# Attention and two MoE layers in one program: head pairs interleaved over partitions, filler products at the start, one half-block slice

## The chip, the core and the metric

The program runs on one core of a Trainium2 chip. Its engines work side by side, each through its own instructions in order: TensorE (PE; PEld is its weight load), VectorE (DVE), ScalarE (ACT), GpSimd (POOL) and SyncE (SP, which here only issues DMAs). They wait for each other by semaphores. The metric is the device time of one execution in microseconds.

## The reference

Four batches of eight heads attend in chunks of 32 queries: each chunk sees 8 memory slots, 16 keys to its left, its own 32 and 8 to its right. Two expert layers without routing follow.

```python
for c in range(nc):                                   # attention, chunk by chunk
    k_full = np.concatenate([mem_k, k_ctx], axis=2)   # 8 + up to 56 keys
    scores = scale * np.matmul(q_c, k_full.transpose(0, 1, 3, 2))
    a = np.exp(scores - scores.max(-1)); a = a / (a.sum(-1) + 1e-9)
    out[:, :, chunk] = np.matmul(a, v_full)
x = out as (3072 tokens, 512)
h = np.maximum(x @ w_in, 0);  x = (s * h * h + b) @ w_out        # d_ff 2048
h = x @ w_in2;  out = (h * sigmoid(1.702 * h)) @ w_out2
```

## The kernel before

**Attention.** The 3072 tokens are 24 tiles of 128. `attend(t)` (line 368) builds one tile's steps. It loads `q` (line 380) and, with two DMAs each, `kbd` and `vbd` (line 384): these hold the keys and values of two heads block by block, head 0 of a pair on partitions 0 to 63 in half 0 of the tile, head 1 on 64 to 127 in half 1, and the other two quarters are zeros, filled once at the start (line 248). So one product with 128 rows gives the scores of both heads: 16 small products (line 392). VectorE takes the maximum (`top`, line 405) and subtracts it (`less`, line 409), ScalarE exponentiates (line 414), TensorE transposes (`pp`, line 419), the result is copied to `pt` (line 211), 16 products give the values (`o`, line 436), VectorE sums and inverts (`total`, lines 427 to 429) and scales to `xn` (line 442), TensorE transposes back (`xx`, line 448), and the block's input is split in a high and a low part, `xh` (line 211) and `xl` (line 460). Four tiles make a block of 512 tokens, six blocks in all.

**The two layers.** Weights come as 64-bit words in 32 column blocks per layer (16 `w_in`, 16 `w_out`); `prep` (line 295) loads one into `st` (line 304) and takes it apart into a high part (`wih`, `woh`) and a low part (`wil`, `wol`) on ScalarE and VectorE (lines 311 to 342). `step` (line 521) takes one column block j for one block of tokens: 12 hidden products into `ph` (lines 537 to 539), the gate on ScalarE and VectorE (lines 545 to 569), 12 output products into `acc` (line 584). The first `LEAD` = 2 column blocks of block 0 are done in halves of 256 tokens: first half (tiles 0 and 1) of j=0 and j=1, then second half (tiles 2 and 3) of both. `VISITS` then sets which blocks pass which j; block 1 follows block 0's first five.

**Order.** `Plan` (line 46) holds every step with its engines, durations and dependences, and lays them out in time on a model of the engines; the order in which it picks them is the order in which the instructions are written. Buffers with tags delay a step until an earlier holder's users are done. `plan.op` makes each step that takes a tagged buffer wait for the step that took it last. In line 271 ten products of a zero tile with itself (`warm`) are put first on TensorE.

Of the kernel before, what the change touches and what calls it, by code (L numbers as in the profile page):

```python
# [32 lines left out]
WARM = 10  # L33
LEAD = 2
NLATE = 4
# [10 lines left out]
class Plan:  # L46


    DMA_START, DMA_END = 1.1, 1.0

    def __init__(self):
        self.ops, self.users, self.tags, self.last, self.soon = [], {}, {}, {}, set()

# [3 lines left out]
    def op(self, need, engines, fn, after=(), alloc=(), uses=()):  # L57
        n = len(self.ops)
        after = list(after)
        for tag, _ in alloc:  # L60
            if tag not in ("a0", "u"):
                if tag in self.last:
                    after.append(self.last[tag])
                self.last[tag] = n
        self.ops.append((need, engines, fn, after, list(alloc), list(uses)))
        for h in uses:
            self.users.setdefault(h, []).append(n)
        return n

    def order(self):  # L70
# [8 lines left out]
        dma_free = 0.0  # L79
        waits = [len(o[3]) for o in ops]  # L80
        outs = [[] for _ in ops]
        for i, o in enumerate(ops):
            for d in o[3]:
                outs[d].append(i)
# [6 lines left out]
        for i in range(len(ops) - 1, -1, -1):  # L91
            need, engines = ops[i][:2]
            due = [late[o] - min(engines.values()) - WAKE for o in outs[i]]
            if "pe" in engines or not due:
                due = [marks[min(bisect.bisect_left(marks, (need, -1.0)), len(marks) - 1)][1]] if "pe" in engines else [
                    marks[min(bisect.bisect_left(marks, (need, -1.0)), len(marks) - 1)][1] - min(engines.values())]
            if i in self.soon:
                due.append(marks[min(bisect.bisect_left(marks, (need, -1.0)), len(marks) - 1)][1])
            late[i] = min(due)

# [9 lines left out]
        def ready(i, e):  # L110
            t = max(free[e], free["act"]) if e == "aq" else free[e]
            for d in ops[i][3]:
                gap = 0.0 if (ran[d] == e and e in ("pe", "sp")) else WAKE
                t = max(t, ends[d] + (gap if e != "none" else 0.0))
            for tag, _ in ops[i][4]:
                bufs, given = self.tags[tag]
                if len(given) >= bufs:
                    h = given[-bufs]
                    for u in self.users.get(h, ()):
                        if ends[u] is None:  # L120
                            return None
                        t = max(t, ends[u] + WAKE)
            return t
# [49 lines left out]
        self.span = max(ends)  # L173
        return chosen


@with_exitstack
def attention_moe_moe(ctx: ExitStack, tc: tile.TileContext, q_t, k_w, v_w, w_in1, w_out1, s_b, w_in2, w_out2, out):
# [26 lines left out]

    plan = Plan()
    op = plan.op
    T = {}
# [46 lines left out]
    o_cold = op(-999, {"dve": 0.2}, chill, alloc=[("r", "cold")])  # L255
    o_ident = op(-200, {"pool": 0.5}, lambda e: make_identity(nc, ident))
    o_zero = {}
    for i in range(2):
        for n in range(2):
            o_zero[i, n] = [  # L260
                op(-150 + 10 * i + n, {"dve": 1.1}, lambda e, x=kvs[i][n][0:64, 1]: fill(e, x, 0.0)),
                op(-150 + 10 * i + n, {"pool": 0.9}, lambda e, x=kvs[i][n][64:128, 0]: fill(e, x, 0.0)),
            ]
# [28 lines left out]
    o_open = {}  # L292
    last = {}

    def prep(i):
# [44 lines left out]
        def rest(e):  # L340
# [3 lines left out]
        st, u = ("st", i), ("u", i)  # L344
        a = op(need, {"sp": 1.9}, load, after=[last[x] for x in ("load",) if x in last], alloc=[("st", st)])
        c = op(need, {"act": 0.67}, low, after=[a], uses=[st])
        b = op(need, {"act": 0.67} if m == 0 else {"act": 0.67, "dve": 0.36}, absolute, after=[a] + [last[x] for x in ("abs",) if x in last] + o_open.get(pool, []),
               alloc=[("u", u), (pool + tag, w)], uses=[st])
# [5 lines left out]
        f = op(need, {"dve": 0.62}, rest, after=[d], uses=[u])  # L354
        last["load"], last["abs"] = a, b
        o_w[w] = (d, f)
# [11 lines left out]
    def attend(t):  # L368
# [13 lines left out]
        def load(x, src, j):  # L382
            h = slice(64 * j, 64 * j + 64)
            return lambda e: (nc.sync if e == "sp" else nc.scalar).dma_start(
                out=x[h, j].rearrange("p a c s -> p (a c s)"), in_=src[t, h])

# [20 lines left out]
        def less(e):  # L407
            T["e", t] = pool.tile([P, H, SLOTS], F32, tag="e", name="e")
            nc.vector.tensor_tensor(  # L409
                out=T["e", t], in0=T["sc", t], in1=T["top", t].to_broadcast([P, H, SLOTS]), op=ALU.subtract  # L410
            )
# [4 lines left out]
        def turn(e):  # L416
            pp = T["pp", t] = ps_a.tile([P, HP, P], F32, tag="a", name="pp")
            for a in range(HP):
                nc.tensor.transpose(pp[:, a, :], T["e", t][:, 2 * a:2 * a + 2, :].rearrange("p h s -> p (h s)"), ident)  # L419

# [4 lines left out]
        def total(e):  # L425
            den = T["den", t] = pool.tile([P, H, 1], F32, tag="den", name="den", bufs=2)
            nc.vector.tensor_reduce(out=den, in_=T["e", t], op=ALU.add, axis=AX.X)
            nc.vector.tensor_scalar_add(out=den, in0=den, scalar1=1e-9)
# [33 lines left out]
        ps, pt, pv, px = [at_a[f, t] for f in "STVX"]  # L462
        lq = op(ps, {"sp": 0.95}, load_q, alloc=[("q" + g, ("q", t))])
        war = [o_s[prior]] if prior is not None else []
        near = [] if t < 2 else [t - 2] if t <= max(EARLY) else [t - 2, t - 1] if t == max(EARLY) + 1 else [t - 1]
        turns, vals, backs = [[o[x] for x in near] for o in (o_t, o_v, o_b)]
        lk = [op(ps, {"aq" if j and t < 8 else "sp": 0.9 if t < 8 else 1.2}, load(kb, k_w, j), after=war) for j in range(2)]
        s = o_s[t] = op(ps, {"pe": 1.05}, scores, after=[lq] + lk + zk + turns, alloc=[("a0", ("sc", t))], uses=[("q", t)])
# [8 lines left out]
        war = [o_v[prior]] if prior is not None else []  # L477
        lv = [op(pv, {"aq" if j and t < 8 else "sp": 0.9 if t < 8 else 1.2}, load(vb, v_w, j), after=war) for j in range(2)]
        o = o_v[t] = op(pv, {"pe": 0.97}, values, after=[d] + lv + zv + backs, alloc=[("a0", ("o", t))], uses=[("pt", t)])
# [41 lines left out]
    def step(i):  # L521
# [72 lines left out]
        for k in range(KT):  # L594
            after = ready + (list(o_split[b, k]) if m else [])
            if d is not None:
                after.append(d)
            d = op(at_h[i], {"pe": dur}, hid(k), after=after, alloc=[("h", ("h", i))] if k == 0 else [],
                   uses=[("x", m, b), win])
# [92 lines left out]

    with tc.manual_schedule():
        for i, e in plan.order():
            plan.ops[i][2](e)
        for x in list(managers)[::-1]:
# [6 lines left out]
def _layouts(q, k, v, mem_k, mem_v, moe_w_in, moe_w_out, moe_s, moe_b, moe2_w_in, moe2_w_out):  # L703
# [17 lines left out]

    q_t = q.reshape(B, HP, 2, TPB, P, D).transpose(0, 3, 2, 5, 1, 4)
    k_w = windows(k, mem_k).transpose(0, 3, 2, 6, 1, 4, 5)
# [30 lines left out]
```

## Time and profile before

| | us |
|---|---|
| median of 3 runs (1158.6 to 1161.57) | 1158.94 |
| profiled execution | 1155.9 |
| its span, first to last instruction | 1154.1 |
| TensorE busy in the span | 1135.5 |
| VectorE busy | 554.4 |
| ScalarE busy | 449.5 |
| mean granted clock of TensorE | 0.989 |

Busy is the time in which an engine had an instruction under way; a product's record covers its pipeline, so neighbours overlap, and the pace is read from start to start. The granted clock is in shares of 2.4 GHz. A mean over the whole span hides its stages: attention of the first eight tiles and the first weights fill the first 80 us.

### The profile page before, as it was taken

What the parts mean: (1) busy time and instruction counts of PE and PEld (TensorE: products, weight loads), DVE (VectorE), ACT (ScalarE), POOL (GpSimd) and SP (SyncE); (2) the same over time, 40 slices, a digit from 0 to 9 for tenths busy, and PEclk for the clock granted to TensorE, in tenths of its full rate; (3) what the DMA queues carried; (4) which work ended last, traced back from release to release, by engine and by line L of the source; (5) the groups of instructions that cost most, each with busy time, mean ns of one, the idle gap of its engine ahead of it and who ended that gap; (6) DMA issues with size and microseconds to landing.
All of it is one profiled execution on the core that took longest, in us unless ns stands there. A gap on an engine that the chain in (4) does not pass through costs nothing.

```text
span 1154.1 us, 15714 instructions
## 1 busy us (share of the span) xinstructions
PE 1135.5 (98%) x6404; PEld 936.5 (81%) x6404; DVE 554.4 (48%) x991; ACT 449.5 (39%) x758; POOL 4.4 (0%) x10
## 2 busy tenths in 40 slices
PE   6899999999999999999999999999999999999998
PEld 5778888888888888888888888888888888888887
DVE  6799983444333434449999822324323223222221
ACT  3679764333334334345555332232222222222222
POOL 1000000000000000000000000000000000000000
PEclk6999999999999999999999999999999999999999
DMA  9974452323113214213444200111001000000000
GB/s 227 246 205 145 129 153 78 89 64 92 47 34 96 69 42 110 65 56 124 132 148 162 93 1 1 37 37 43 31 1 39 35 1 1 37 1 1 36 1 37
DMA packets 30647, 84.89 MB, mean 74 GB/s; under 512 B 3952, under 2 KB 3952, under 8 KB 30576
## 3 DMA queue, kind: packets, MB, share of 16 engines
q1 hardware_dynamic: 29296, 79.71, 23.9%
q10 hardware_dynamic: 1280, 4.20, 1.6%
q8 instruction: 50, 0.82, 0.3%
q14 instruction: 21, 0.17, 0.0%
HBM read 71.30 MB, written 12.58 MB: 73 GB/s over the span
## 4 chain that ended last, share of the span: by engine, by line
PE 94%; DMA 3%; DVE 1%; ACT 1%; issue 0%; SPq 0%; DVEq 0%; ACTq 0%
PE acc L584 44%; PE ph L537 15%; PE ph L538 15%; PE ph L539 15%; PE o L436 2%; PE sc L392 2%; DMA st<-w_in 1%; PE pp L419 1%; DMA st<-w_out 1%; PE xx L448 1%; DMA kbd<-k_w 1%; DMA q<-q_t 1%; DVE e L409 0%; DVE top L405 0%; ACT u L311 0%
## 5 line engine op out<-in xcount | busy, mean ns | idle before, releaser
L537 PE MATMUL ph<-xh,wih 128*128 128x512 f32 (+1 forms) x776 | 305.7, 394 | 0.0
L538 PE MATMUL ph<-xl,wih 128*128 128x512 f32 (+1 forms) x776 | 301.0, 388 | 0.0
L539 PE MATMUL ph<-xh,wil 128*128 128x512 f32 (+1 forms) x776 | 300.9, 388 | 0.0
L569 DVE TENSOR_TENSOR gl<-r,gh 128x512 fp32r<-128x512 f32 (+1 forms) x194 | 132.8, 684 | 213.8 <-ACT gh L565 213.6
L565 ACT CAST gh<-r 128x512 fp32r<-128x512 f32 (+1 forms) x194 | 119.9, 618 | 261.9 <-PE acc L584 250.8
L537 PEld LDWEIGHTS ph<-xh,wih 128*128 128x128 f32 x776 | 146.5, 189 | 33.1 <-issue 4.7
L539 PEld LDWEIGHTS ph<-xh,wil 128*128 128x128 f32 x776 | 146.2, 188 | 30.3 <-DVE wil L342 0.3
L538 PEld LDWEIGHTS ph<-xl,wih 128*128 128x128 f32 x776 | 146.5, 189 | 28.1
L561 DVE TENSOR_TENSOR r<-ph,r 128x512 f32<-128x512 f32 x96 | 66.3, 691 | 180.8 <-ACT r L547 180.5
L584 PE MATMUL acc<-gh,woh 128*128 128x512 f32 (+1 forms) x392 | 151.5, 386 | 0.0
L584 PE MATMUL acc<-gl,woh 128*128 128x512 f32 (+1 forms) x392 | 150.9, 385 | 0.2 <-DVE gl L569 0.2
L584 PE MATMUL acc<-gh,wol 128*128 128x512 f32 (+1 forms) x392 | 151.0, 385 | 0.0
L584 PE MATMUL acc<-woh,gh 128*128 128x512 f32 x384 | 149.4, 389 | 0.0
L584 PE MATMUL acc<-wol,gh 128*128 128x512 f32 x384 | 149.4, 389 | 0.0
L584 PE MATMUL acc<-woh,gl 128*128 128x512 f32 x384 | 149.4, 389 | 0.0
L547 ACT ACTIVATE r<-ph 128x512 f32<-128x512 f32 x96 | 57.4, 598 | 209.4 <-PE ph L539 208.6
L545 ACT ACTIVATE r<-ph 128x512 f32<-128x512 f32 (+1 forms) x98 | 57.8, 590 | 143.0 <-PE ph L539 136.6
L559 DVE TENSOR_SCALAR r<-r,sb 128x512 f32<-128x512 f32 x86 | 46.8, 545 | 118.0 <-ACT r L554 117.3
L584 PEld LDWEIGHTS acc<-gh,woh 128*128 128x128 f32 x392 | 73.6, 188 | 15.3 <-issue 0.8
L584 PEld LDWEIGHTS acc<-gl,woh 128*128 128x128 f32 x392 | 73.7, 188 | 14.9 <-DVE gl L569 0.4
L584 PEld LDWEIGHTS acc<-gh,wol 128*128 128x128 f32 x392 | 73.7, 188 | 14.6
L584 PEld LDWEIGHTS acc<-woh,gl 128*128 128x128 f32 x384 | 72.1, 188 | 15.0
(62 smaller groups left out, 891.5 us busy)
## 6 DMA issues: line engine op xcount, KB each, us to landing
st<-w_in SPq DMA_DIRECT2D x32, 512.0 KB, 3.5
st<-w_out SPq DMA_DIRECT2D x32, 512.0 KB, 3.9
kbd<-k_w SPq DMA_DIRECT2D x40, 256.0 KB, 4.9
vbd<-v_w SPq DMA_DIRECT2D x40, 256.0 KB, 4.2
q<-q_t SPq DMA_DIRECT2D x24, 256.0 KB, 5.2
xf<-y SPq DMA_DIRECT2D x6, 1024.0 KB, 5.2
out<-y SPq DMA_DIRECT2D x20, 256.0 KB, 2.2
y<-y SPq DMA_DIRECT2D x16, 256.0 KB, 2.1
```

What stands on the lines that cost most here:

```text
L392: nc.tensor.matmul(sc[r, 2 * a:2 * a + 2, :], T["q", t][:, a, r], kb[:, :, a, c, :], start=True, stop=True)
L436: nc.tensor.matmul(o[r, 2 * a:2 * a + 2, :], T["pt", t][:, a, r], vb[:, :, a, c, :], start=True, stop=True)
L537: nc.tensor.matmul(ph, wh, xh, start=(k == 0), stop=False)
L538: nc.tensor.matmul(ph, wh, xl, start=False, stop=False)
L539: nc.tensor.matmul(ph, wl, xh, start=False, stop=(k == KT - 1))
L545: nc.scalar.activation(out=a, in_=T["ph", i], func=AF.Relu)
L547: nc.scalar.activation(out=a, in_=T["ph", i], func=AF.Sigmoid, scale=GATE)
L559: nc.vector.tensor_scalar(out=a, in0=a, scalar1=sb[:, 0:1], scalar2=sb[:, 1:2], op0=ALU.mult, op1=ALU.add)
L561: nc.vector.tensor_tensor(out=a, in0=T["ph", i], in1=a, op=ALU.mult)
L565: nc.scalar.copy(out=T["g", i][0], in_=T["r", i])
L569: nc.vector.tensor_tensor(out=gl, in0=T["r", i], in1=gh.bitcast(F32), op=ALU.subtract)
L584: nc.tensor.matmul(o, lt, rh, start=fresh and x == 0, stop=(done and x == 2))
```

## The change

1. **Interleaving.** Head 0 of a pair now lies on the even partitions and head 1 on the odd ones, in `q`, `kbd`, `vbd` and the transposed exponents. The loads write every second partition (`x[j::2, j]`), the zero fill covers all 128 partitions of both halves, and the loads of tiles 0 and 1 wait for it. To have the transposes come out interleaved, the tile `e` is stored with the two heads alternating word by word: `less` writes it in steps of two words, `total` reads it so.
2. **Fillers.** Where the plan leaves TensorE idle before the first hidden product, products of the zero tile with itself are written, one per 0.24 us of the planned gap.
3. **LEAD = 1.** Only j=0 of block 0 is done in two halves.
4. **The plan.** A step with a tagged buffer no longer waits for the end of the step that took it last, only for its start; loads and first steps of different weights are no longer chained; planned durations of loads change, the zero fills and the identity get other due times, and the `vbd` loads of tiles 0 and 1 are all issued by SyncE.

```diff
-LEAD = 2
+LEAD = 1
...
+    BEAT = 0.24
...
-        after = list(after)
+        behind = []
         for tag, _ in alloc:
             if tag not in ("a0", "u"):
                 if tag in self.last:
-                    after.append(self.last[tag])
+                    behind.append(self.last[tag])
                 self.last[tag] = n
...
                 t = max(t, ends[d] + (gap if e != "none" else 0.0))
+            for d in ops[i][6]:
+                t = max(t, starts[d])
...
-        return chosen
+        full, clock = [], 0.0
+        for i, e in chosen:
+            if e == "pe":
+                idle = min(starts[i], starts[self.first]) - clock
+                if idle > 0.3:
+                    full.append((None, int(idle / self.BEAT)))
+                clock = ends[i]
+            full.append((i, e))
+        return full
...
-                op(-150 + 10 * i + n, {"dve": 1.1}, lambda e, x=kvs[i][n][0:64, 1]: fill(e, x, 0.0)),
-                op(-150 + 10 * i + n, {"pool": 0.9}, lambda e, x=kvs[i][n][64:128, 0]: fill(e, x, 0.0)),
+                op(-150 + 10 * i + n, {"dve": 1.1}, lambda e, x=kvs[i][n][:, 1]: fill(e, x, 0.0)),
+                op(-150 + 10 * i + n, {"pool": 0.9}, lambda e, x=kvs[i][n][:, 0]: fill(e, x, 0.0)),
...
-        a = op(need, {"sp": 1.9}, load, after=[last[x] for x in ("load",) if x in last], alloc=[("st", st)])
+        a = op(need, {"sp": 1.55}, load, alloc=[("st", st)])
...
-                out=x[h, j].rearrange("p a c s -> p (a c s)"), in_=src[t, h])
+                out=x[j::2, j].rearrange("p a c s -> p (a c s)"), in_=src[t, h])
...
-            T["e", t] = pool.tile([P, H, SLOTS], F32, tag="e", name="e")
+            T["e", t] = pool.tile([P, HP, SLOTS, 2], F32, tag="e", name="e")
             nc.vector.tensor_tensor(
-                out=T["e", t], in0=T["sc", t], in1=T["top", t].to_broadcast([P, H, SLOTS]), op=ALU.subtract
+                out=T["e", t].rearrange("p a s h -> p a h s"), in0=T["sc", t].rearrange("p (a h) s -> p a h s", h=2),
+                in1=T["top", t].rearrange("p (a h) o -> p a h o", h=2).to_broadcast([P, HP, 2, SLOTS]), op=ALU.subtract
...
-            nc.vector.tensor_reduce(out=den, in_=T["e", t], op=ALU.add, axis=AX.X)
+            nc.vector.tensor_reduce(
+                out=den.rearrange("p (a h) o -> p a (h o)", h=2), in_=T["e", t].rearrange("p a s h -> p a h s"), op=ALU.add, axis=AX.X)
...
-        lk = [op(ps, {"aq" if j and t < 8 else "sp": 0.9 if t < 8 else 1.2}, load(kb, k_w, j), after=war) for j in range(2)]
+        lk = [op(ps, {"aq" if j and t < 8 else "sp": 0.8}, load(kb, k_w, j), after=war + (zk if t < 2 else [])) for j in range(2)]
...
         for i, e in plan.order():
-            plan.ops[i][2](e)
+            if i is not None:
+                plan.ops[i][2](e)
+                continue
+            if idle is None:
+                idle = ps_acc.tile([P, 512], F32, tag="acc3", name="idle")
+            for _ in range(e):
+                nc.tensor.matmul(idle[:, :P], T["cold"], T["cold"], start=True, stop=True)
...
-    q_t = q.reshape(B, HP, 2, TPB, P, D).transpose(0, 3, 2, 5, 1, 4)
+    q_t = q.reshape(B, HP, 2, TPB, P, D).transpose(0, 3, 5, 2, 1, 4)
```

**The order that comes of it.** First place: TensorE from the program's start to the scores of tile 2. Before (`kbd_93` and `kbd_95` are the two key tiles, used by even and odd tiles; numbers tell buffers apart):

```order
L269 MATMUL warm_106<-cold_99 128x128 x10
L392 MATMUL sc_151<-kbd_93,q_117 32x128 x16
L392 MATMUL sc_179<-kbd_95,q_124 32x128 x16
L419 MATMUL pp_200<-ident_91,e_176 128x128 x4
L436 MATMUL o_215<-vbd_94,pt_210 32x128 x16
L419 MATMUL pp_239<-ident_91,e_213 128x128 x4
L436 MATMUL o_255<-vbd_96,pt_249 32x128 x16
L448 MATMUL xx_275<-ident_91,xn_251 128x128 x4
L448 MATMUL xx_288<-ident_91,xn_282 128x128 x4
L392 MATMUL sc_296<-kbd_93,q_170 32x128 x16
```

After, the same stretch to the second tile's values (the two transposes back and the scores of tile 2 follow, with three fillers between each):

```order
L717 MATMUL idle_105<-cold_99 128x128
L282 MATMUL warm_107<-cold_99 128x128 x10
L717 MATMUL idle_105<-cold_99 128x128 x9
L403 MATMUL sc_162<-kbd_93,q_102 32x128 x16
L717 MATMUL idle_105<-cold_99 128x128 x8
L403 MATMUL sc_206<-kbd_95,q_121 32x128 x16
L431 MATMUL pp_230<-ident_91,e_195 128x128 x4
L717 MATMUL idle_105<-cold_99 128x128 x10
L449 MATMUL o_262<-vbd_94,pt_238 32x128 x16
L431 MATMUL pp_285<-ident_91,e_249 128x128 x4
L717 MATMUL idle_105<-cold_99 128x128 x5
L449 MATMUL o_309<-vbd_96,pt_294 32x128 x16
```

The attention steps stand in the same order; 39 fillers stand among them, 10 before the first scores.

Second place: SyncE's first loads. Before:

```order
L304 DMA st_102<-w_in1 128x1024
L380 DMA q_117<-q_t 128x512
L384 DMA kbd_93<-k_w 64x1024
L380 DMA q_124<-q_t 128x512
L384 DMA kbd_95<-k_w 64x1024
L384 DMA vbd_94<-v_w 64x1024
L384 DMA vbd_96<-v_w 64x1024
```

After:

```order
L391 DMA q_102<-q_t 128x512
L316 DMA st_118<-w_in1 128x1024
L391 DMA q_121<-q_t 128x512
L395 DMA kbd_93<-k_w 64x1024
L316 DMA st_127<-w_out1 128x1024
L395 DMA kbd_95<-k_w 64x1024
L316 DMA st_136<-w_in1 128x1024
L395 DMA vbd_94<-v_w 64x1024 x2
```

The first key load moves from third to fourth, the second weight from ninth to fifth, and a third weight is put ahead of the first values. On ScalarE's queue stood two key and two value halves; there now stand the two key halves.

Third place: VectorE from the first `xl` of block 0 on. Before (`st_139` is the second weight, `st_237` the third):

```order
L460 TENSOR_TENSOR xl0_285<-xx_275,xh0_284 128x4x128
L460 TENSOR_TENSOR xl0_285<-xx_288,xh0_284 128x4x128
L342 TENSOR_TENSOR wol_245<-u_246,woh_244 128x512
L405 TENSOR_REDUCE top_322<-sc_296 128x8
L409 TENSOR_TENSOR e_331<-sc_296,top_322 128x512
L317 TENSOR_SCALAR u_340<-u_340 128x512
L405 TENSOR_REDUCE top_367<-sc_342 128x8
L325 TENSOR_SCALAR u_340<-u_340 128x512
L409 TENSOR_TENSOR e_374<-sc_342,top_367 128x512
L329 ISA u_340<-st_237,u_340 128x1024
```

After (`st_136` is the third weight, `st_181` the fourth):

```order
L345 SCALAR_TENSOR_TENSOR u_245<-st_136,u_245 128x512
L473 TENSOR_TENSOR xl0_339<-xx_329,xh0_338 128x4x128
L329 TENSOR_SCALAR u_302<-u_302 128x512
L473 TENSOR_TENSOR xl0_339<-xx_345,xh0_338 128x4x128
L354 TENSOR_TENSOR wil_244<-u_245,wih_243 128x512
L416 TENSOR_REDUCE top_388<-sc_359 128x8
L337 TENSOR_SCALAR u_302<-u_302 128x512
L420 TENSOR_TENSOR e_402<-sc_359,top_388 128x4x2x64
L341 ISA u_302<-st_181,u_302 128x1024
L416 TENSOR_REDUCE top_425<-sc_404 128x8
```

VectorE reaches the second `xl` with the third weight nearly done and the fourth begun; before, it finished the second there.

## Rows read from the trace of the kernel before

**Rows 1.** The page, part 1: busy us, share of the span, instructions.

```profile
PE 1135.5 (98%) x6404; PEld 936.5 (81%) x6404; DVE 554.4 (48%) x991; ACT 449.5 (39%) x758; POOL 4.4 (0%) x10
```

**Rows 2.** Windows: us, busy by engine (x instructions), granted clock, DMA share, GB/s.

```profile
10.00:20.00 10.00, 7.00 (x102) 5.43 (x98) 5.30 (x12) 2.31 (x4) 0.00 (x0) 0.50 1.06 233
...
50.00:60.00 10.00, 9.37 (x108) 7.40 (x109) 9.65 (x24) 7.24 (x15) 0.00 (x0) 1.00 0.97 265
...
60.00:80.00 20.00, 18.69 (x230) 14.80 (x229) 18.45 (x37) 15.16 (x27) 0.00 (x0) 1.00 0.84 222
...
300.00:600.00 300.00, 300.00 (x1864) 246.76 (x1857) 165.17 (x314) 126.56 (x212) 0.00 (x0) 1.00 0.30 85
```

**Rows 3.** Timeline of TensorE: start us, us, engine, line, operation, out<-in, idle before.

```profile
1.06 4.64 PE L269 MATMUL warm<-cold 128*128 128x128 f32 x20 [1.06 <-DVE cold L248]
...
9.85 1.93 PE L392 MATMUL sc<-kbd,q 128*32 128x128 f32 x32 [4.15 <-DMA kbd<-k_w]
...
27.70 0.58 PE L537 MATMUL ph<-xh,wih 128*128 128x256 f32 x1
...
30.31 1.08 PE L392 MATMUL sc<-kbd,q 128*32 128x128 f32 x32
...
43.25 0.28 PE L537 MATMUL ph<-xh,wih 128*128 128x256 f32 x1
...
44.69 0.28 PE L537 MATMUL ph<-xh,wih 128*128 128x256 f32 x1
...
47.23 0.39 PE L584 MATMUL acc<-gh,woh 128*128 128x256 f32 x1
...
81.73 0.48 PE L537 MATMUL ph<-xh,wih 128*128 128x512 f32 x1
...
90.01 0.39 PE L537 MATMUL ph<-xh,wih 128*128 128x512 f32 x1
...
95.45 0.39 PE L537 MATMUL ph<-xh,wih 128*128 128x512 f32 x1
```

**Rows 4.** Windows, the microsecond in which the clock comes back.

```profile
29.00:30.00 1.00, 1.00 (x7) 1.00 (x7) 0.59 (x2) 0.69 (x3) 0.00 (x0) 0.53 1.06 236
```

**Rows 5.** Timeline of VectorE.

```profile
11.89 0.17 DVE L399 MEMSET sc<- 32x128 f32 x1 [2.57 <-PE sc L392]
...
25.97 0.69 DVE L460 TENSOR_TENSOR xl<-xx,xh 128x512 fp32r<-128x512 f32 x1 [0.18 <-ACT xh L211]
...
41.55 1.28 DVE L460 TENSOR_TENSOR xl<-xx,xh 128x512 fp32r<-128x512 f32 x2
...
80.59 1.28 DVE L460 TENSOR_TENSOR xl<-xx,xh 128x512 fp32r<-128x512 f32 x2
```

**Rows 6.** Lines by form, VectorE, 0 to 84 us: busy, mean ns, idle before.

```profile
L333 DVE SCALAR_TENSOR_TENSOR u<-st,u 128x512 uint32<-128x512 uint32 x10 | 6.8, 676 | 0.1
...
L409 DVE TENSOR_TENSOR e<-sc,top 128x512 f32<-128x512 f32 x9 | 6.1, 683 | 0.1
...
L325 DVE TENSOR_SCALAR u<-u 128x512 uint32<-128x512 uint32 x11 | 4.6, 420 | 0.1
...
L248 DVE MEMSET kbd<- 64x1024 f32 x2 | 1.8, 912 | 0.3 <-issue 0.3
...
L399 DVE MEMSET sc<- 32x128 f32 x2 | 0.3, 165 | 2.7 <-PE sc L392 2.6
...
L248 DVE MEMSET cold<- 128x128 f32 x1 | 0.2, 165 | 0.8 <-PEq L743 0.8
```

**Rows 7.** Windows: attention loads alone, then weights alone.

```profile
300.00:310.00 10.00, 10.00 (x91) 8.38 (x84) 6.14 (x11) 3.13 (x6) 0.00 (x0) 1.00 0.56 131
...
600.00:610.00 10.00, 10.00 (x46) 8.27 (x45) 8.42 (x18) 6.17 (x12) 0.00 (x0) 1.00 0.62 212
```

**Rows 8.** Chain of waits: start us, us, what; tile 0's first key load.

```profile
1.66 8.05 DMA kbd<-k_w
```

**Rows 9.** Line 384, 0 to 45 us: landing of the key and value loads.

```profile
DMA to landing us min/median/max: 5.6/8.7/10.3
```

More of the change, by code (lines that the diff above doesn't have):

```diff
@@ L49 @@
     DMA_START, DMA_END = 1.1, 1.0
+    BEAT = 0.24
     def __init__(self):
-        self.ops, self.users, self.tags, self.last, self.soon = [], {}, {}, {}, set()
+        self.ops, self.users, self.tags, self.last, self.soon, self.due = [], {}, {}, {}, set(), {}
     def tag(self, name, bufs):
@@ L62, in op @@
                 if tag in self.last:
-                    after.append(self.last[tag])
+                    behind.append(self.last[tag])
                 self.last[tag] = n
-        self.ops.append((need, engines, fn, after, list(alloc), list(uses)))
+        self.ops.append((need, engines, fn, list(after), list(alloc), list(uses), behind))
         for h in uses:
@@ L79, in order @@
         dma_free = 0.0
-        waits = [len(o[3]) for o in ops]
+        waits = [len(o[3]) + len(o[6]) for o in ops]
         outs = [[] for _ in ops]
         for i, o in enumerate(ops):
-            for d in o[3]:
+            for d in o[3] + o[6]:
                 outs[d].append(i)
@@ L98, in order @@
                 due.append(marks[min(bisect.bisect_left(marks, (need, -1.0)), len(marks) - 1)][1])
-            late[i] = min(due)
+            late[i] = self.due.get(i, min(due))
         def push(i):
@@ L206, in attention_moe_moe @@
     plan = Plan()
+    plan.first = None
     op = plan.op
@@ L255, in attention_moe_moe @@
     o_cold = op(-999, {"dve": 0.2}, chill, alloc=[("r", "cold")])
-    o_ident = op(-200, {"pool": 0.5}, lambda e: make_identity(nc, ident))
+    plan.due[o_cold] = -1000.0
+    o_ident = op(-135, {"pool": 0.5}, lambda e: make_identity(nc, ident))
     o_zero = {}
@@ L292, in attention_moe_moe @@
     o_open = {}
-    last = {}
     def prep(i):
@@ L344, in prep @@
         st, u = ("st", i), ("u", i)
-        a = op(need, {"sp": 1.9}, load, after=[last[x] for x in ("load",) if x in last], alloc=[("st", st)])
+        a = op(need, {"sp": 1.55}, load, alloc=[("st", st)])
         c = op(need, {"act": 0.67}, low, after=[a], uses=[st])
-        b = op(need, {"act": 0.67} if m == 0 else {"act": 0.67, "dve": 0.36}, absolute, after=[a] + [last[x] for x in ("abs",) if x in last] + o_open.get(pool, []),
+        b = op(need, {"act": 0.67} if m == 0 else {"act": 0.67, "dve": 0.36}, absolute, after=[a] + o_open.get(pool, []),
                alloc=[("u", u), (pool + tag, w)], uses=[st])
@@ L354, in prep @@
         f = op(need, {"dve": 0.62}, rest, after=[d], uses=[u])
-        last["load"], last["abs"] = a, b
         o_w[w] = (d, f)
@@ L418, in turn @@
             for a in range(HP):
-                nc.tensor.transpose(pp[:, a, :], T["e", t][:, 2 * a:2 * a + 2, :].rearrange("p h s -> p (h s)"), ident)
+                nc.tensor.transpose(pp[:, a, :], T["e", t][:, a].rearrange("p s h -> p (s h)"), ident)
         def turned(e):
@@ L462, in attend @@
         ps, pt, pv, px = [at_a[f, t] for f in "STVX"]
-        lq = op(ps, {"sp": 0.95}, load_q, alloc=[("q" + g, ("q", t))])
+        lq = op(ps, {"sp": 0.8}, load_q, alloc=[("q" + g, ("q", t))])
         war = [o_s[prior]] if prior is not None else []
@@ L477, in attend @@
         war = [o_v[prior]] if prior is not None else []
-        lv = [op(pv, {"aq" if j and t < 8 else "sp": 0.9 if t < 8 else 1.2}, load(vb, v_w, j), after=war) for j in range(2)]
+        lv = [op(pv, {"aq" if j and 2 <= t < 8 else "sp": 0.8}, load(vb, v_w, j), after=war + (zv if t < 2 else [])) for j in range(2)]
         o = o_v[t] = op(pv, {"pe": 0.97}, values, after=[d] + lv + zv + backs, alloc=[("a0", ("o", t))], uses=[("pt", t)])
@@ L597, in step @@
                 after.append(d)
+            if plan.first is None:
+                plan.first = len(plan.ops)
             d = op(at_h[i], {"pe": dur}, hid(k), after=after, alloc=[("h", ("h", i))] if k == 0 else [],
@@ L693, in attention_moe_moe @@
     with tc.manual_schedule():
+        idle = None
         for i, e in plan.order():
-            plan.ops[i][2](e)
+            if i is not None:
[5 more added lines that the diff above has]
+                nc.tensor.matmul(idle[:, :P], T["cold"], T["cold"], start=True, stop=True)
         for x in list(managers)[::-1]:
```

## The prediction

> **What bounds the kernel now.** The page comes first: TensorE counts as busy for 98% of the span [rows 1]. The stage windows split that. From 300 to 600 us TensorE is busy in every microsecond while VectorE is busy 165 of 300; from 50 to 80 us VectorE is at 9.65 of 10 and 18.45 of 20 [rows 2]. So the long part runs at matmul pace, 0.227 us per 512-column product (24 products from 90.01 to 95.45, rows 3), which nothing here touches. What can be won lies before the point from which TensorE runs without a gap: the first product of block 1, at 81.73 [rows 3].
>
> The third view is TensorE in order of time [rows 3]. Ten warm-up products take 4.64 us and end at 5.70; then TensorE stands until 9.85 for the first scores, and by the window 10 to 20 the granted clock is 0.50, the 1.2 GHz level [rows 2]. In the window 29 to 30 its mean is still 0.53 [rows 4]. A tile's scores take 1.93 us at the lower level and 1.08 at the upper [rows 3]. The fourth view is VectorE [rows 5]. Between the first scores (11.89) and the second `xl` (end 26.66) it needs 14.8 us for 19 instructions whose durations [rows 6] add to 10.0: it waits there, for TensorE, ScalarE and DMAs. Between 42.83 (end of the fourth `xl`) and 81.87 (end of the eighth) it needs 39.0 us for 74 instructions that add to 40.4, since neighbours overlap: there VectorE sets the pace. The fifth is DMA: from 10 to 20 us its share is full [rows 2]; key, value and query loads move 131 GB/s at a share of 0.56, weights 212 GB/s at 0.62 [rows 7], so 234 against 342 GB/s at a full share. The first half of tile 0's keys lands 8.05 us after its issue [rows 8], and in the first 45 us such loads take 5.6 to 10.3 us [rows 9].
>
> **The change, step by step**, on the profiled execution: 1155.9 us, of which the span is 1154.1. That is 3.0 us under the median of the runs shown; I carry the difference over to the median.
>
> *First scores.* The kbd loads now wait for zero fills of 128 partitions instead of standing beside fills of 64. VectorE fills 128 columns in 0.165 us on 32 and on 128 partitions alike [rows 6], so I price a fill as before, 0.91; twice that is the upper bound and adds 1.8 us for the two of kbd. Behind the waiting load SyncE holds w_out and the next kbd, ScalarE the first weight's absolute value; none is due earlier than the scores. On SyncE the load is now fourth, behind q, w_in and q. What can stand before its end is 1.31 MB on this queue and 0.52 MB on ScalarE's, 1.83 MB; before, it was 1.05 and 1.05 MB in 8.05 us. At the same rate 7.0 us; if the 0.79 MB of keys among it move at 342 instead of 234 GB/s, 1.1 us less, 5.9. Issued at about 2.1 (three issues of some 0.45 from 0.75 on), it lands at 8.0 to 9.1. TensorE must by then have done 20 products of zeros (the ten of before and ten fillers), 0.46 each at the lower level and 0.26 at the upper (by 1.08 to 1.93), so 5.2 to 9.3 us from 1.06 on: 6.3 to 10.4. I take 8.5 for the first scores, in the middle of both; 9.85 before.
>
> That rate rests on a load that no row shows, 64 rows on every second partition. The Trainium skill, SBUF — State Buffer, section "Door 1: The DMA port swizzle", says that 64 partitions in a row reach half of the 16 ports (196 GB/s at 1 MiB, against 328 for 128 partitions), and by its table the even partitions alone would reach all of them. The rows fit its first part, 234 against 342. The same page, under "Can I just issue two DMAs to hit both halves?", holds that only one transfer over all 128 partitions gets there. By the table the load lands 5.9 us after its issue and by the second section 7.0 (estimates from the rows above).
>
> *First scores to first hidden product.* TensorE gets 29 more fillers between the attention steps (8, 10, 5, 3 and 3), so I take the upper clock here. Then VectorE is the chain: 26 instructions stand from the first scores to the second `xl`, 16 at 0.69, 5 at 0.42, 5 small ones at 0.17 to 0.2: 14.0 us, with 0.03 between them 14.9. Before, 19 took 14.8 with 4.8 us of waiting; the seven more are weight work that stood later. The first scores end at 9.6, plus 0.1 to wake VectorE: the second `xl` ends at 24.6, and there the first hidden product can go on; before, 27.70. Gain 3.1. Bounds: with the waiting share of before (14.8 to 10.0) it would be 20.7 us and the gain gone; with the overlap of the later stretch (39.0 to 40.4) 13.6, gain 4.4. I take 14.9, near the upper end, because the seven fill waits that were there. The fillers stand where TensorE waits for VectorE and cost nothing; the ten before the first value product (2.6 us) may hold it a little, but the `xn` that needs it has some 4 us of other VectorE work ahead of it. Without that cover, up to 2.
>
> *To the scores of tile 4.* Before: the first half-block of j=0 and 1, then the second of both; scores of tile 4 end where the row at 47.23 begins. After: both halves of j=0, then j=1 whole; the products are the same otherwise. VectorE has 26 instructions to the fourth `xl`, 14.6 us, with gaps 15.4: it ends at 40.0. The second half of j=0 (1.44, from 43.25 to 44.69 in rows 3) and j=1 (12 full products, 2.72) end at 44.3, with the scores of tile 4 done already. Gain at this point 2.9. No filler is put in here, so the clock may fall; as VectorE is the chain I cost that at nothing, but where it covers the 4.2 us of products at the end, it costs up to 4.2.
>
> *To block 1.* By the fourth `xl` VectorE will have done 56 instructions where it had done 46; what is left to the eighth adds to 38.3 instead of 40.4, times 0.97 is 37.0, so it ends at 77.0. TensorE took 34.5 us from 47.23 to 81.73, of which 0.63 and 1.31 were waits (rows 2, 50 to 80). It now has 2.1 us more ahead of block 1 (24 full products for 24 half ones, one transpose group less): 44.3 + 34.5 + 2.1 = 80.9 with all the waits, 79.0 with none, when VectorE is 2 us ahead. I let three quarters go, 1.5. Half of those 24 are j=1's output products, 12 full for 24 half: 2.72 for 2.88, another 0.15.
>
> *The strided exponent tile.* `less` writes every second word, `total` reads every second. A VectorE read of every second word shows no price: 676 ns on line 333 against 683 for the contiguous line 409 [rows 6]. A strided write on VectorE is not in the trace: between 0 and a doubling of its columns (0.69 less 0.17, so 0.52). I take 0, the nearest row being the read.
>
> *The rest.* After 81.73 the products and the evacuations are the same; 300 to 600 shows no gap in which a moved load could show. Cost 0; a load that now comes too late there would be the price, and none is bounded by a row.
>
> Sum: 2.9 + 1.5 + 0.15 = 4.55 us. 1155.9 becomes 1151.3, and against the median 1158.94 **1154.4 us**.
>
> **Rivals.**
> *The loads do not get faster.* For it: each is still 64 descriptors of 4 KB. Against: rows 7, where the covered partitions differ most. Then the first scores come at 9.1 at the earliest, later loads queue as before at a share already full, and only their order is gained, about 1 us: 1158.
>
> *Late first scores, clock down.* If the first kbd takes the worst of now, 10.3 us from its issue, scores begin at 12.4; TensorE has stood 2 to 6 us and the clock may fall as it did before 9.85. Scores then take 1.93 and fillers 0.46 each. VectorE's chain ends at 12.4 + 2.0 + 14.9 = 29.3 instead of 24.6, and the 4.7 us take the whole gain: 1159.1. Against it: fewer bytes stand ahead than before.
>
> *Slower: the strided accesses double.* Place: `less` and `total` on VectorE, the chain up to block 1. Price: 0.52 each, two a tile, eight tiles, 8.3 us. It decides from 0.57 a tile on, where the gain is gone, and from 1.0 it is slower by 0.3%. 1154.4 + 8.3 = 1162.7. Against it speaks the read of line 333.
>
> **How the numbers follow.** My forecast has 0.63, with a range of its own from 1150 to 1157.5: overlap in the first two stretches (1.3 each) and the last 0.4 of waits give 1151.4, first scores at 7 rather than 8.5 the rest; a clock fall at half its 4.2 gives 1156.5. Loads not faster 0.15, late scores 0.13, strides 0.09. The range takes in the two middle cases and stops short of the third: 1150 to 1159. A measurement of this kernel can tell about 0.3% from no change, 3.5 us, so under 1155.4 is faster. Of the forecast 0.53 lies there and 0.10 within; of the first rival 0.03 and 0.12; of the second 0.03 and 0.08, with 0.02 slower; of the third 0.01 within and 0.08 slower. Faster 0.59, same 0.31, slower 0.10.
>
> **What would show it.** First scores near 8.5 at about 1.08 us a tile; granted clock 1.00 from 10 to 25; the second `xl` ending near 24.6, the fourth near 40, the eighth near 77; block 1 begun near 79.4 with no gap behind it; loads of the first 45 us landing in 4 to 7 us; `less` and `total` at 0.69. Wrong would be: first scores beyond 11, VectorE idle for more than 3 us between the first scores and the fourth `xl`, a subtract well over 0.69, or a TensorE gap after block 1 began.

## The result and the profile after

| | before | after |
|---|---|---|
| median, us | 1158.77 (6 runs) | 1147.69 (6 runs, 1146.02 to 1150.18) |
| ratio, 95% interval | | 0.9911, 0.9887 to 0.9935 |
| the same on a second chip | 1158.13 (15 runs) | 1147.45; 0.991, 0.9882 to 0.9938 |
| profiled run; its span | 1155.9; 1154.1 | 1148.27; 1146.5 |

The change is worth 10 to 11 us by the medians and the ratios, and 7.6 us between the two traces. The prediction said 4.55 us, 1154.4, and a range down to 1150: right in sign, less than half of the size by the medians. The lines below are of the trace after; their line numbers are those of the changed kernel.

First the windows of the trace after (us, busy by engine and instructions for TensorE, its weight load, VectorE, ScalarE and GpSimd; granted clock, DMA share, GB/s), against [rows 2, 4].

```profile
8.00:12.00 4.00, 3.51 (x68) 3.23 (x72) 2.59 (x6) 2.04 (x4) 0.00 (x0) 1.00 1.03 414
...
10.00:20.00 10.00, 10.00 (x157) 9.03 (x157) 9.83 (x22) 6.47 (x12) 0.00 (x0) 1.00 0.87 317
...
28.00:36.00 8.00, 7.18 (x83) 5.89 (x84) 6.46 (x14) 3.81 (x8) 0.00 (x0) 0.57 0.89 301
...
60.00:80.00 20.00, 20.00 (x202) 15.54 (x202) 18.20 (x36) 14.35 (x26) 0.00 (x0) 1.00 0.51 153
300.00:600.00 300.00, 300.00 (x1820) 246.66 (x1819) 167.80 (x316) 134.76 (x225) 0.00 (x0) 1.00 0.28 89
```

A full DMA share moves 414 GB/s (from 8 to 12 us) where the kernel before had 233 at 1.06. VectorE, at 5.30 of 10 between 10 and 20 us before, is at 9.83. The clock is up there, and down later, from 28 to 36. The long part is as it was.

TensorE in order of time, against [rows 3] (start us, us, engine, line, operation, idle before):

```profile
8.49 1.08 PE L403 MATMUL sc<-kbd,q 128*32 128x128 f32 x32 [0.93 <-DVE u L345]
...
22.43 0.39 PE L550 MATMUL ph<-xh,wih 128*128 128x256 f32 x1
...
26.81 0.66 PE L431 MATMUL pp<-ident,e 128*128 128x128 f32 x4 [1.69 <-ACT e L426]
28.14 1.46 PE L449 MATMUL o<-vbd,pt 128*32 128x128 f32 x32 [0.68 <-ACT pt L223]
...
31.32 1.93 PE L449 MATMUL o<-vbd,pt 128*32 128x128 f32 x32 [0.68 <-ACT pt L223]
...
39.58 0.40 PE L550 MATMUL ph<-xh,wih 128*128 128x512 f32 x1
...
42.34 0.60 PE L431 MATMUL pp<-ident,e 128*128 128x128 f32 x4
...
54.52 0.65 PE L461 MATMUL xx<-ident,xn 128*128 128x128 f32 x4 [1.16 <-DVE xn L455]
...
76.66 0.50 PE L550 MATMUL ph<-xh,wih 128*128 128x512 f32 x1
```

The order of the work differs, so start times alone don't compare. I take the time that TensorE has lost at a point: the time, less the products done by then at their pace at the upper clock (0.227 us for 512 columns, 0.12 for 256, 1.01 for a tile's scores or values, 0.44 for four transposes; zero products count as nothing).

| lost on TensorE up to | before | after | gain | forecast |
|---|---|---|---|---|
| the first scores (9.85; 8.49) | 9.85 | 8.49 | 1.4 | 1.35 |
| the first hidden product (27.70; 22.43) | 20.9 | 15.6 | 5.3 | 3.1 |
| j=0 and 1 hidden, tile 4 scored (47.23; 42.34) | 27.4 | 22.7 | 4.7 | 2.9 |
| block 1 (81.73; 76.66) | 31.9 | 24.9 | 7.0 | 4.55 |

Behind block 1 nothing more is lost in either trace. Of the 0.6 us between these 7.0 and the 7.6 between the traces, some 0.3 are the 48 half products that became 24 full ones (5.76 against 5.45 us, each counted here at its own pace); the rest is not placed. After 54.52 TensorE has no gap at all; the chain that ended last runs on it unbroken from there.

VectorE in order of time, against [rows 5]:

```profile
9.68 0.17 DVE L410 MEMSET sc<- 32x128 f32 x1 [1.38 <-PE sc L403]
...
18.76 0.68 DVE L341 CUSTOM_DVE_ANT_0 u<-st,u 128x1024 uint16<-128x1024 uint16 x1
19.36 0.68 DVE L455 TENSOR_TENSOR xn<-o,den 128x512 f32<-128x512 f32 x1
19.96 0.68 DVE L345 SCALAR_TENSOR_TENSOR u<-st,u 128x512 uint32<-128x512 uint32 x1
20.56 0.68 DVE L473 TENSOR_TENSOR xl<-xx,xh 128x512 fp32r<-128x512 f32 x1
...
21.49 0.68 DVE L473 TENSOR_TENSOR xl<-xx,xh 128x512 fp32r<-128x512 f32 x1
...
37.41 0.69 DVE L473 TENSOR_TENSOR xl<-xx,xh 128x512 fp32r<-128x512 f32 x1 [0.26 <-ACT xh L223]
...
75.39 0.68 DVE L473 TENSOR_TENSOR xl<-xx,xh 128x512 fp32r<-128x512 f32 x1
```

A record lasts 0.68 us, but the next one starts 0.60 after it. The second, fourth and eighth `xl` end at 22.17, 38.10 and 76.07; forecast 24.6, 40.0 and 77.0. The lines by form (VectorE, 0 to 84 us) and the landing of key and value loads to 45 us, against [rows 6, 9]:

```profile
L439 DVE TENSOR_REDUCE den<-e 128x8 f32<-128x512 f32 x8 | 5.4, 679 | 0.9 <-ACT e L426 0.9
L420 DVE TENSOR_TENSOR e<-sc,top 128x512 f32<-128x512 f32 x8 | 5.4, 676 | 0.0
L260 DVE MEMSET kbd<- 128x1024 f32 x2 | 1.8, 912 | 0.3 <-issue 0.3
```

```profile
DMA to landing us min/median/max: 3.2/5.5/6.9
```

And a window of the long part in which only key, value and query loads run, against [rows 7]; at a full share its rate would be 338 GB/s, where the kernel before had 234:

```profile
290.00:300.00 10.00, 10.00 (x105) 8.22 (x103) 5.00 (x10) 3.45 (x6) 0.00 (x0) 1.00 0.39 132
```

### The profile page after: what moved, and what is told of

Same layout as the page of the kernel before. It is cut to its first block, busy times and chain, and to the rows that moved or that the text cites. A ratio compares the mean times of both kernels' runs of the same rounds, so it can differ in the third digit from the quotient of the medians.

```text
span 1146.5 us, 15816 instructions
## 1 busy us (share of the span) xinstructions
PE 1136.6 (99%) x6458; PEld 939.3 (82%) x6458; DVE 546.6 (48%) x978; ACT 455.2 (40%) x766; POOL 4.3 (0%) x10
## 4 chain that ended last, share of the span: by engine, by line
PE 95%; ACT 0%; issue 0%; DVE 0%
PE acc L597 45%; PE ph L550 15%; PE ph L551 15%; PE ph L552 15%; PE o L449 2%; PE sc L403 1%; PE xx L461 1%; PE pp L431 1%; ACT y L223 0%; DVE u L337 0%
## 5 line engine op out<-in xcount | busy, mean ns | idle before, releaser
L597 PEld LDWEIGHTS acc<-gh,woh 128*128 128x128 f32 x388 | 73.3, 189 | 14.9 <-issue 0.4
L597 PEld LDWEIGHTS acc<-gh,wol 128*128 128x128 f32 x388 | 73.1, 188 | 14.9
L597 PEld LDWEIGHTS acc<-woh,gh 128*128 128x128 f32 x384 | 72.1, 188 | 15.0
```

Of the source, the lines that this page charges most:

```text
L597: nc.tensor.matmul(o, lt, rh, start=fresh and x == 0, stop=(done and x == 2))
```

## Experiments

Of the changed kernel, one part was taken back at a time. **Without the fillers:**

```diff
-            for _ in range(e):
-                nc.tensor.matmul(idle[:, :P], T["cold"], T["cold"], start=True, stop=True)
```

> The changed kernel without the idle matmuls; every other instruction in the same order (the zero products after the warm-up and between the first attention steps are left out; they feed nothing). Theory 'clock': without them TensorE stands between the steps, the granted clock falls to 0.50 as it did in the kernel before, and the two scores (1.93 for 1.08), two value products (1.93 for 1.08) and the transposes of tiles 0 and 1 stand on the chain: first hidden product 3 to 4.5 us later than 22.43, total 1150.5 to 1152.5. Theory 'transfers': the steps wait for data and VectorE, so the lower clock is hidden: first hidden product 0 to 1 us later, total 1147.5 to 1149.

Measured 1147.6, ratio to before 0.9913 (0.9898 to 0.9928): no difference. The windows of this run:

```profile
8.00:20.00 12.00, 8.89 (x124) 6.79 (x128) 9.18 (x22) 7.10 (x12) 0.00 (x0) 0.50 0.93 318
20.00:28.00 8.00, 7.47 (x107) 5.87 (x100) 6.41 (x12) 3.84 (x9) 0.00 (x0) 0.71 1.00 366
28.00:36.00 8.00, 5.38 (x90) 4.27 (x89) 7.86 (x18) 4.69 (x9) 0.00 (x0) 1.00 0.89 310
```

```profile
25.02 0.39 PE L550 MATMUL ph<-xh,wih 128*128 128x256 f32 x1
```

Theory 'clock' came near at the first hidden product: it is 2.6 us later, at 25.0, with 2.6 us more lost, where the theory had 3 to 4.5. It had the end wrong, and there theory 'transfers' is right: the clock comes back and is up from 28 to 36, where the changed kernel falls to 0.57, and with the hidden products of j=1 done the two have lost 22.4 and 22.7. The fillers move the low clock to a later and shorter stretch; they don't remove it.

**The interleaving undone** (layouts of queries and exponents too):

```diff
-                out=x[j::2, j].rearrange("p a c s -> p (a c s)"), in_=src[t, h])
+                out=x[h, j].rearrange("p a c s -> p (a c s)"), in_=src[t, h])
```

> The changed kernel with the interleaving alone undone: keys and values go to partitions 0 to 63 and 64 to 127, queries and the exponent tile are laid out as before; fillers, half-block slice and the planner's rules stay. Theory 'transfers': the loads fall back from over 400 to 200 to 270 GB/s in the first 30 us, the first scores come 1 to 2 us later and every later attention step of the first two tiles waits again: total 1152 to 1155. Theory 'clock': the transfers are hidden behind fillers and VectorE but for the first load: 1.4 us later at most, total 1147.5 to 1149.

1161.94, ratio 1.004 (1.0025 to 1.0055): slower than the kernel before, some 14 us over the changed one and beyond even the first theory. Its window, three of its TensorE rows, and the landing of its key and value loads to 45 us:

```profile
8.00:12.00 4.00, 3.04 (x48) 2.70 (x48) 2.07 (x5) 0.92 (x2) 0.00 (x0) 1.00 1.03 249
```

```profile
8.96 1.08 PE L403 MATMUL sc<-kbd,q 128*32 128x128 f32 x32 [0.98 <-DMA kbd<-k_w]
...
28.01 1.08 PE L403 MATMUL sc<-kbd,q 128*32 128x128 f32 x32 [3.71 <-DMA kbd<-k_w]
...
34.77 0.66 PE L430 MATMUL pp<-ident,e 128*128 128x128 f32 x4 [3.04 <-ACT e L425]
```

```profile
DMA to landing us min/median/max: 6.0/9.2/11.8
```

249 against 414 GB/s at the same share of 1.03, with the clock up in both (these windows hold weight and query loads too), and a median of 9.2 us to landing against 5.5. The first scores still come at 8.96: there the rate is worth only 0.5 us. What it feeds is the second pair of tiles and the weights.

**Two half-block slices:**

```diff
-LEAD = 1
+LEAD = 2
```

> The changed kernel with two half-block slices (j = 0 and 1) as before; all else stays. If the one slice is worth what the prediction's small term says, 0.15 us: 1147.5 to 1148.5. If the half products of j = 1 fill the gap of 1.69 us at 25.1 and the clock falls later or not at all, it is faster: 1145 to 1147. If the single slice carries the gain (less VectorE and ScalarE work ahead of the scores of tile 4), 1149.5 to 1152.

1155.65, ratio 0.9988 (0.9977 to 0.9999): 8 us lost, beyond the third theory. The trace puts most of them, 5.82, in one place. TensorE, and VectorE's order ahead of it:

```profile
82.86 1.11 PE L431 MATMUL pp<-ident,e 128*128 128x128 f32 x4 [5.82 <-ACT e L426]
```

```profile
76.24 0.68 DVE L345 SCALAR_TENSOR_TENSOR u<-st,u 128x512 uint32<-128x512 uint32 x1
...
79.66 0.68 DVE L416 TENSOR_REDUCE top<-sc 128x8 f32<-128x512 f32 x1
...
81.46 0.69 DVE L420 TENSOR_TENSOR e<-sc,top 128x512 f32<-128x512 f32 x1
```

Tile 7's `top` and `less` stand behind weight steps; up to the eighth `xl` VectorE has 151 instructions here, 130 in the changed kernel. That looks like the order, not the slice; three runs further down bear on it.

**The planner's old rules and costs** (chains and costs of the weight loads, waits for a predecessor's end, due times):

```diff
-                    behind.append(self.last[tag])
+                    after.append(self.last[tag])
...
-        a = op(need, {"sp": 1.55}, load, alloc=[("st", st)])
+        a = op(need, {"sp": 1.9}, load, after=[last[x] for x in ("load",) if x in last], alloc=[("st", st)])
```

> The changed kernel with the planner's rules and costs of before (a tile waits for its buffer's predecessor to end, weight loads and absolute values in one chain, SyncE costs 1.9, 0.95, 0.9 and 1.2, the second half of the first value loads on ScalarE, identity and cold fill with their old due times); interleaving, fillers and one slice stay. Theory 'order': the seven weight instructions that VectorE does between the first scores and the second xl stand later again, so block 1 begins 1 to 3 us later: 1149 to 1151. Rival: the order alone is worth nothing once transfers and clock are right: 1147 to 1148.5.

1149.08, ratio 0.9929 (0.9913 to 0.9945), as theory 'order' has it, at its lower end; the interval overlaps that of the changed kernel (0.9887 to 0.9935), so the 1.4 us between their medians are not clear of noise. VectorE reaches the eighth `xl` after 113 instructions, at 67.5, but the weight steps put off are then late for TensorE:

```profile
68.73 0.50 PE L598 MATMUL acc<-gl,woh 128*128 128x512 f32 x1 [1.74 <-DVE gl L583]
```

Then one part alone on the kernel before. **The interleaving alone**, with its fills and their waits:

> The kernel before with the interleaving alone (keys, values, queries, exponent tile; zero fills of 128 partitions and the loads waiting for them), no fillers, two half-block slices, the old rules of the planner. Theory 'transfers': with the fillers worth nothing (1147.6 without them) and the loss at two slices (1155.7) made by the new rules' order for tile 7, the interleaving alone brings nearly all: 1147.5 to 1150.5. Rival 'slice': the one half-block slice is worth some 8 us in itself, as the run with two suggests: 1154 to 1157.

1150.39, ratio 0.9952 (0.9936 to 0.9968): the number of theory 'transfers', at its upper end, but not its words: 5.5 us are about half of the gain, not nearly all. **With one slice** (`LEAD = 1`) on top:

> The kernel before with the interleaving and one half-block slice, old rules, no fillers. With the interleaving alone it took 1150.4, and with fillers and one slice under the old rules 1149.1. Theory 'the slice is worth nothing in itself': 1149.5 to 1151, and then the 8 us between one and two slices under the new rules are those rules' order. Rival 'the slice is worth something under any rules': 1146.5 to 1149.

1151.21, ratio 0.9951 (0.9935 to 0.9967): the same ratio as with two slices, 0.2 us beyond the first theory's range and further from the rival's. Under the old rules the slice is worth nothing in itself. So says **no slice at all** in the changed kernel (`LEAD = 0`):

> The changed kernel without any half-block slice: hidden products begin when all four tiles of block 0 are done. Theory 'VectorE paces to the eighth xl': TensorE's work of the half slice (5.8 us) moves behind the fourth tile, where TensorE waits anyway for VectorE, which has no fewer instructions: 1147 to 1150. Rival 'TensorE paces': the 5.8 us are lost where they stood, in the stretch before the scores of tile 4: 1151 to 1153.

1146.59, ratio 0.9917 (0.9903 to 0.993): the ratio of the changed kernel within the noise, 0.4 us under the first theory's range. The 8 us of two slices are thus what the new rules do with them.

**VectorE made longer**, each tile's maximum taken twice:

> The changed kernel with each tile's maximum taken twice on VectorE, one more instruction of 0.6 us pitch in each of the eight tiles ahead of block 1. Theory 'VectorE paces': nearly all of 8 times 0.6 comes out at the end, 3.5 to 5 us: 1151 to 1153. Rival 'transfers or TensorE pace': the instruction falls into VectorE's waits, 0 to 1.5 us: 1147.5 to 1149.5.

1148.74 (1148.07 to 1152.33), ratio 0.9944: by the medians 1.3 us above the changed kernel (the rival's range), by the ratios (0.9944 against 0.991) some 4. In the one trace, of a run of 1152.14, the eighth `xl` ends at 79.46 instead of 76.07, and the span is 3.8 us longer than that of the traced changed kernel: there VectorE paces.

```profile
78.78 0.68 DVE L474 TENSOR_TENSOR xl<-xx,xh 128x512 fp32r<-128x512 f32 x1
```

Four of the six runs took 1148.1 to 1148.9, and none of them was traced; for those it stays open.

**More fillers**, behind the first hidden product too. They are products of the identity with itself, not of zeros as the expectations say; they feed nothing either:

```diff
+        more = {o_s[3]: 6, o_t[2]: 2, o_t[3]: 2}
...
+                for _ in range(more.get(i, 0)):
+                    nc.tensor.matmul(idle[:, :P], ident, ident, start=True, stop=True)
```

> The changed kernel with ten more zero products: six behind the fourth tile's scores, two each behind the transposes of tiles 2 and 3, where TensorE waited 1.69, 0.68 and 0.68 us and after which the clock stood at 0.50 from 28.7 to 35.5. Theory 'the fall moved': the fillers of the first 22 us only put the low clock off to a later stretch, and with the later gaps filled too the clock stays up and the 3.3 us of that stretch go: 1143.5 to 1145.5. Rival: VectorE is the chain there and the low clock costs nothing, or the fillers themselves delay the transposes: 1147 to 1148.5.

1145.63, but a ratio of 0.9911; the run on one chip with the changed kernel had to decide.

> The changed kernel once more, beside the three others of this call on one chip. If the 7.6 us between the two profiled runs is the gain and the 11.1 between the medians is spread: a ratio of 0.9925 to 0.994. If the profile of before was a quick run and the medians tell the gain: 0.989 to 0.992.

> The kernel with ten more zero products once more, now beside the changed kernel on one chip. Theory 'the low clock from 28.7 to 35.5 costs 3.3 us': 2 to 3.3 us below the changed kernel. Rival 'VectorE is the chain there': within 1 us of it.

Changed kernel 1147.45 (1146.73 to 1148.04), more fillers 1145.92 (1144.48 to 1146.74; ratio to before 0.9898, 0.9873 to 0.9922): 1.5 us, between theory and rival. The mean clock is 1.0 in every run of it, and its trace has no fall where the changed kernel had 0.57:

```profile
28.00:36.00 8.00, 6.90 (x121) 5.81 (x123) 7.86 (x19) 4.93 (x11) 0.00 (x0) 1.00 0.90 303
```

So by the medians the fall that the first fillers only put off costs 1 to 2 us. Between the traces it is more: the two of the changed kernel span 1146.5 and 1146.2 us, the two with more fillers 1143.0 and 1143.9, which is 2.3 to 3.5 less and near the theory's 3.3. The medians may mix runs with and without the fall: of the changed kernel's first six, those with a mean clock of 0.995 and 0.996 took 1148.3 to 1150.2 us and those with 0.999 and 1.0 took 1146.0 to 1147.1. The changed kernel's own ratio here, 0.991, lies where the medians tell its gain, though its interval (0.9882 to 0.9938) reaches into the other outcome.

**The exponent of tile 2 ahead of a weight** on ScalarE, the fillers behind tile 3's scores taken out:

```diff
-        c = op(need, {"act": 0.67}, low, after=[a], uses=[st])
+        c = op(need, {"act": 0.67}, low, after=[a] + ([o_e[2]] if i == 4 else []), uses=[st])
```

(and the same wait for `absolute`).

> The kernel with more fillers, and on ScalarE the exponent of tile 2 put ahead of the third input weight's two conversions, behind whose load it stood until 25.3; the six fillers behind the scores of tile 3 go. Theory 'the wait on ScalarE is on the chain': the transposes of tile 2 begin at 25.1 instead of 26.4 and 0.7 to 1.5 us come out at the end: 1143.5 to 1145 where the fillers alone give 1145.6. Rival: VectorE has the same list ahead of block 1 and paces, 0 to 0.5 us.

1144.41 (1144.03 to 1145.1), ratio 0.9887 (0.9863 to 0.991), 1.5 us below the fillers alone: at the upper end of the theory, and the fastest of all. The transposes of tile 2 begin at 25.35, with the fillers alone at 27.34, and 0.8 us of lost time is gone by 36 us (19.9 against 20.7). But the added wait changes the plan behind it too: VectorE ends the eighth `xl` at 68.0 after 123 instructions, where it was 73.5 after 130. So it is not shown that all of the 1.5 us come from this wait. ScalarE in the trace after, then here:

```profile
25.30 0.66 ACT L323 ACTIVATE u<-st 128x512 f32<-128x512 f32 x1 [3.35 <-DMA st<-w_in]
25.86 0.37 ACT L558 ACTIVATE r<-ph 128x256 f32<-128x256 f32 x1
26.13 0.62 ACT L426 ACTIVATE e<-e 128x512 f32<-128x512 f32 x1
```

```profile
24.39 0.39 ACT L558 ACTIVATE r<-ph 128x256 f32<-128x256 f32 x1 [2.19 <-PE ph L552]
24.68 0.62 ACT L426 ACTIVATE e<-e 128x512 f32<-128x512 f32 x1
```

**Where the kernel before spreads.** Its 49 runs beside these kernels lie between 1152.28 and 1161.57, median 1157.05; the one traced, 1155.9, is among the quicker quarter. Three more traces of it:

> The kernel before, unchanged, for a second trace of it. If the 3 us between its profiled run and its median lie in the transfers of the first 45 us, a run near 1158 shows the first hidden product or the scores of tile 4 later by 2 to 4 us, and the same distance from there on. If they lie in the clock, it shows the low level later than 29.94 or again behind 40.18. If they lie in the long part, the distance grows after 81.73.

> As the run before this one: the kernel before, a third trace, for the place of its spread; the same three outcomes.

> As the two runs before this one: the kernel before, a fourth trace, for the place of its spread; the same three outcomes.

1160.66, 1157.52 and 1155.14. TensorE's lost time up to 108 us is 36.6, 33.5 and 31.2, and 31.9 in the trace read before; the spans differ by the same amounts, so the whole spread lies ahead of that point. In the slowest and in the second:

```profile
11.38 1.94 PE L392 MATMUL sc<-kbd,q 128*32 128x128 f32 x32 [5.89 <-DMA kbd<-k_w]
...
77.34 1.08 PE L392 MATMUL sc<-kbd,q 128*32 128x128 f32 x32 [2.04 <-DMA q<-q_t]
```

```profile
62.60 1.08 PE L392 MATMUL sc<-kbd,q 128*32 128x128 f32 x32 [3.85 <-DVE xl L460]
```

```profile
60.83 0.66 ACT L311 ACTIVATE u<-st 128x512 f32<-128x512 f32 x1 [4.03 <-DMA st<-w_out]
```

The waits of 5.89 and 2.04 were 4.15 [rows 3] and 0.36 in the trace before. Behind the 3.85 stands a wait of 4.03 on ScalarE for a `w_out` load. All three are late loads. They are not the whole difference: in the slowest trace the clock is also up from 20 to 32 us and at 0.52 from 32 to 42, where the trace read before had 0.83, and how much that costs was not separated.

## Why the prediction was wrong

**The base: wrong.** "I carry the difference over to the median": these 3.0 us aren't a constant of the two kernels. Three further traces put such differences ahead of block 1, in late loads for the most part; and the three runs were high, for over 49 runs the median is 1157.05, 1.15 above the traced run. The changed kernel's profiled run lies 0.6 us above its median. Of the miss of 6.7 us (1154.4 to 1147.7) this is 3.6.

**First scores: right**, 8.49 for 8.5. But that step gave the faster rate most of its worth, and it is the place where it matters least (8.96 without it).

**To the first hidden product: mis-sized; the step that failed on the traced run.** "14.0 us, with 0.03 between them 14.9": the 26 instructions took 12.5 (9.68 to 22.17), because neighbours that wait for nothing start 0.60 after one another. I had that overlap from VectorE's later stretch as the bound for the largest gain, 13.6, and chose the side where it waits; 12.5 is below even that bound. The waits, 4.8 us before, were for loads and slow products and went nearly all. Of the 3.1 us missing between the traces 2.2 arise here; 0.4 are lost again by the scores of tile 4, 0.7 come from more waits saved on the way to block 1, and 0.6 lie outside the table.

**Rate: right.** 342 GB/s at a full share was assumed for the key loads; read in the same way, from attention loads alone, it is 338 (132 at 0.39). The crowded window from 8 to 12 us had more, 414, with all kinds of loads in it. The Trainium skill, SBUF — State Buffer, section "Door 1: The DMA port swizzle", lets 64 partitions in a row reach 8 of 16 ports, with 218 GB/s as their limit against 436 for all 16; by its table the even partitions reach all. The 414 lie under the second limit; the 249 lie above the first, in a window that also holds loads over all 128 partitions. The sentence under "Can I just issue two DMAs to hit both halves?", that only one transfer over all 128 partitions gets there, does not hold here: loads of 64 rows on alternate partitions got 338 and, among others, 414.

**Fillers: wrong in kind.** That they "cost nothing" was right; that their gain stays was not. The fall of which the step to the scores of tile 4 says "I cost that at nothing" came at 28.7 and gave the gain back; it is worth 1.5 us by the medians and 2.3 to 3.5 between traces, inside the bound of 4.2 that was stated. It works against the miss, not for it.

**To block 1: right in kind.** Waits saved: 2.3 against 1.5; only the one of 1.16 at 54.52 is left. VectorE was ahead by the eighth `xl`, as forecast, but by 0.6 us (76.07 before 76.66) and not by 2.

**Half to full products, 0.15: below what can be told** (no slice, one slice, two under the old rules all agree). **Strided tile, 0: right**, 676 and 679 ns. **The rest, 0: right**, the same lost time from block 1 to the end.

**Rivals.** Loads not faster: no. Late first scores: no. Strides: no. The forecast was the right case, and its range was too narrow, since all its bounds came from one trace.

**Whose gain it is.** Interleaving alone: ratio 0.9952, about 5.5 us. The new rules with one slice on top (the run without fillers): 0.9913, another 4.5. The slice by itself: nothing. The fillers: nothing on top of the new rules (0.9913 without, 0.9911 with them). Under the old rules, with the interleaving and one slice, two runs differ in the fillers alone: 0.9951 without and 0.9929 with them, 2.5 us, from two chips and with intervals that overlap. So the rules are worth 4.5 us without fillers and 2.1 with them (0.9929 to 0.9911), the fillers perhaps 2.5 without the rules and nothing with them: the two win part of the same time, and which waits they share is not shown. The new rules need the fast loads: without them the kernel is slower than before.

## What to carry to other kernels

Read where a transfer lands before asking how long it takes: with two loads of 64 rows on alternate partitions instead of halves, the first microseconds moved 1.7 times as much (414 against 249 GB/s), and waits for key loads (3.71 us at the third tile with halves) went. The runs spread less too: six of the changed kernel lie within 4.2 us, the six of the kernel before beside them within 7.7. Price a queue of instructions that wait for nothing by start to start, not by record. A single trace hides a distribution: where runs spread by 0.8%, the change may remove part of the spread itself.

## What the hardware showed that was not expected

- Loads on alternate partitions: 414 GB/s at a share of 1.03 (weights and queries among them), on halves 249 at 1.03; alone 132 at 0.39, on halves 131 at 0.56.
- Full-width VectorE instructions start 0.60 us apart where each record says 0.68.
- Filling TensorE's gaps early moved the stretch at the lower clock and shortened it, without a gain in the end: 8 to 24 us without fillers, 28.7 to 35.5 with them; with the gaps behind it filled too, none, and 1.5 us less.
